# The beginning of attention: order of the first loads, reductions, casts and fillers

## The chip, the cores and the metric

The kernel runs on one core of a Trainium2 chip. A core has TensorE (PE, matrix products), VectorE (DVE), ScalarE (ACT), GpSimd (POOL) and SyncE (SP, which issues most DMAs). Each engine takes its own instructions in order; semaphores order them across engines. The metric is device time of one execution in microseconds. Before the change it was 1071.04 us, the median of three runs (1067.99 to 1071.36).

## The reference, cut to what matters

Three layers follow each other. Attention has a pooled part (q, k, v averaged over 4 neighbours) and a local part (a band of 3 neighbours to each side); then a dense layer with softplus, then a soft mixture of 8 experts.

```python
q_d, k_d, v_d = (x.reshape(B, H, Sd, 4, D).mean(axis=3) for x in (q, k, v))   # B 2, H 8, S 576, D 64
out_up = np.repeat(sm_attn(q_d, k_d, v_d), 4, axis=2)
scores = np.where(mask, scale * q @ k.T, -1e9)                                # mask: |i - j| < 4
out = out_up + softmax(scores) @ v
h = softplus(x @ w_in); x = h @ w_out                                         # 512 -> 2048 -> 512
ye = np.maximum(x @ w1[e], 0) @ w2[e]; out += P[:, e:e+1] * ye                # 8 experts, P from x @ w_gate
```

## The kernel before, in words

Heads are taken in pairs, four pairs p to a batch b. A pair's k is a tile of 128 rows (two heads of 64) by 576 positions. Its q is held twice, once for each head, with the other head's 64 rows blanked with zeros (`blank`), so that one product over 128 rows gives one head's scores. Batch 0's q lies in `q0a` (pairs 0 and 1) and `q0b` (pairs 2 and 3), places that later hold other tensors.

`load_qk` issues a pair's loads (k on SyncE's queue, q's two halves on ScalarE's queue for batch 0). `pool_qk` sums groups of 4: q by one VectorE reduction (`qd`, L250), k by two GpSimd sums (`ks`, L256, and `kd`, L258); ScalarE then scales both. `constants` loads the identity and the mask and casts them to bf16. `load_vd` loads v for pooling, in two halves, and sums each half by two instructions (`vs`, L277, and `vd`, L279), on VectorE for batch 0 and on GpSimd for batch 1. Its raw tiles `vr` share two buffers (tag `raw`) with the weights that `load_raw` loads later. `load_vw` loads v for the local windows.

The attention is cut into units. A pooled unit takes two heads and half of the pooled positions; a local unit takes 116 positions and four heads. Each has four stages: s1 scores (`pd`, or `pl` with the mask added by a product with the identity), a maximum over each row (`nm`, VectorE, L287) and exponentials (`e`, ScalarE, L290); s2 transposes (`ptd`, `ptl`) and a copy by ScalarE; s3 products with v (`pvd`, `pvl`) and the division by the sum; s4 a transpose back (`pxd`, `pxl`) and, in a local unit, the sum of both parts (`xf`) and the split into two parts of x. A unit's first scores of `pooled(0, 0, p)` use pairs 0 and 1 for p = 0 and 2, and pairs 2 and 3 for p = 1 and 3.

`emit` goes through the units; at each one it calls s1 of this unit, s2 of the unit two back, s3 of the one four back and s4 of the one six back. After these calls, counted by n, it calls `warm(1)` for n under 20 and for every fourth n up to 88. `warm` issues matmuls on a tile of zeros whose result nobody reads (fillers), 17 of them at the very start (`WARM`). Some entries in the list of units are other calls, placed by the dictionary `at`: batch 1's loads (`load_second`, at unit 1), batch 1's v and the first weights (`load_rest`, at unit 9), batch 1's pooling, the conversion of weights (`prep` and `from_double`: ScalarE `cm` L126 and `cs` L124, then VectorE), and the first products of the dense layer.

The program's order isn't the order on the engines: a planner goes through the program with simulated times, and on each engine takes the earliest instruction in the program that it holds ready. `tc.issue_after(ins)` ties what the block issues on `ins`'s engine behind `ins`; it holds nothing on other engines.

Of the kernel before, what the change touches and what calls it, by code (L numbers as in the profile page):

```python
# [19 lines left out]
DM = H * D  # L20
# [30 lines left out]
STEP = 2  # L51
WARM, JALL, JN, NJ = 17, 20, 4, 88
GP = 80
# [23 lines left out]
class Net:  # L77
# [9 lines left out]


    def constants(self):
        nc = self.nc  # L90
        self.ident = self.const.tile([P, P], F32, name="ident")
        nc.sync.dma_start(out=self.ident, in_=self.a["ident"])
        self.identb = self.atp.tile([P, P], BF16, tag="identb", name="identb", bufs=1)
        nc.vector.tensor_copy(self.identb, self.ident)
        self.mask = self.atp.tile([P, len(OFF), KW], BF16, tag="mask", name="mask", bufs=1)
        self.maskf = self.convp.tile([P, len(OFF), KW], F32, tag="cm", name="maskf", bufs=1)
        nc.sync.dma_start(out=self.maskf, in_=self.a["mask"])
        nc.vector.tensor_copy(self.mask, self.maskf)
        self.ones = self.const.tile([P, P], F32, name="ones")
        nc.gpsimd.memset(self.ones, 1.0)  # L100
# [94 lines left out]
    def warm(self, n):  # L195
# [7 lines left out]
        for _ in range(n):  # L203
            self.nc.tensor.matmul(ps, lhsT=z[:, 0], rhs=z.to_broadcast([P, 4, P]), start=True, stop=True)

    def attention_pools(self, stack):
        tc = self.tc
        self.convp = stack.enter_context(tc.tile_pool(name="conv", bufs=1, side="right"))
        self.qkp = stack.enter_context(tc.tile_pool(name="qkp", bufs=NPAIR, side="right"))
        self.vwp = stack.enter_context(tc.tile_pool(name="vwp", bufs=3, side="right"))  # L210
        self.atp = stack.enter_context(tc.tile_pool(name="atp", bufs=3, side="right"))
        self.tmp = stack.enter_context(tc.tile_pool(name="tmp", bufs=2, side="right"))
        self.psm = stack.enter_context(tc.tile_pool(name="psm", bufs=2, space=bass.MemoryType.PSUM))
        self.psa = stack.enter_context(tc.tile_pool(name="psa", bufs=6, space=bass.MemoryType.PSUM))
        self.kT, self.qd, self.kd, self.vw, self.vd, self.upT = {}, {}, {}, {}, {}, {}

    def places(self):


        q = self.hp.tile([P, 2, 2, S], F32, tag="h", name="q0a")  # L220
        x = self.xyp.tile([P, 2, 2, S], F32, tag="xy", name="q0b")
        self.qT = {(0, p): (q, x)[p // 2][:, p % 2] for p in range(NPAIR)}
        for t in (q, x):
            self.blank(t, self.nc.vector)

# [4 lines left out]
    def load_qk(self, b, p):  # L230
        nc = self.nc
        if b == 1:
            if p < NPAIR - 1:
                q = self.qkp.tile([P, 2, S], F32, tag="q", name=f"q1{p}", bufs=NPAIR - 1)
            else:
                q = self.accp.tile([P, 2, S], F32, tag="yp1", name="q13")
            self.blank(q, nc.gpsimd)
            self.qT[b, p] = q
        k = self.k1[:, p] if b == 1 else self.qkp.tile([P, S], F32, tag="k", name=f"k{p}")
        nc.sync.dma_start(out=k, in_=self.a["k"][b, p])  # L240
        self.kT[b, p] = k
        for g in range(2):
            rows = slice(g * D, (g + 1) * D)
            (nc.scalar if b == 0 else nc.sync).dma_start(out=self.qT[b, p][rows, g], in_=self.a["q"][b, p][rows])

    def pool_qk(self, b, p):

        nc = self.nc
        qd = self.atp.tile([P, 2, G], F32, tag="qd", name=f"qd{b}{p}", bufs=NPAIR)
        nc.vector.tensor_reduce(  # L250
            out=qd, in_=self.qT[b, p].rearrange("p h (g f) -> p h g f", f=POOLF), op=ALU.add, axis=AX.X
# [5 lines left out]
        kd = self.atp.tile([P, G], F32, tag="kd", name=f"kd{b}{p}", bufs=NPAIR)  # L257
        nc.gpsimd.tensor_tensor(kd, s[:, :, 0], s[:, :, 1], ALU.add)  # L258
        nc.scalar.activation(kd, kd, AF.Copy, scale=SCALE / (POOLF * POOLF))
# [8 lines left out]
    def load_vd(self, b):  # L268
# [3 lines left out]
        for hf in range(2):  # L272
            r = self.rawp.tile([GP, POOLF, DM], F32, tag="raw", name=f"vr{b}{hf}")
            nc.sync.dma_start(out=r, in_=self.a["vp"][b, hf].rearrange("p (f d) -> p f d", f=POOLF))
            s = self.convp.tile([GH, 2, DM], F32, tag=("ch", "cs")[hf], name=f"vs{b}{hf}", bufs=1)
            e = nc.vector if b == 0 else nc.gpsimd
            e.tensor_tensor(s, r[:GH, 0:2], r[:GH, 2:4], ALU.add)  # L277
            sv = s.rearrange("p f (h d) -> p f h d", h=H)
            e.tensor_tensor(vd[:, hf, :, 0:D], sv[:, 0], sv[:, 1], ALU.add)  # L279
        self.vd[b] = vd  # L280
        self.upT[b] = self.atp.tile([P, NPAIR, G], F32, tag="upT", name=f"upT{b}", bufs=2)

    def softmax_exp(self, ps, n, m, k, tag):

        nc = self.nc
        nm = self.atp.tile([m, n], F32, tag="nm" + tag, name="nm")
        nc.vector.tensor_reduce(out=nm, in_=ps, op=ALU.max, axis=AX.X, negate=True)  # L287
        e = self.atp.tile([m, n, k], F32, tag="e" + tag, name="e", bufs=3 if tag == "l" else 2)
        for j in range(n):
            nc.scalar.activation(e[:, j], ps[:, j], AF.Exp, bias=nm[:, j : j + 1])  # L290
        return e

    def pooled(self, b, hf, p):
# [4 lines left out]
        def s1():  # L298
            ps = self.psa.tile([P, 512], F32, tag="a", name="pd")[:GH, : 2 * G].rearrange("p (j k) -> p j k", j=2)
            for j in range(2):  # L300
                nc.tensor.matmul(
                    ps[:, j],
# [7 lines left out]
        def s2():  # L310
# [3 lines left out]
            for j in range(2):  # L314
                for kh in range(2):
                    nc.tensor.transpose(ps[:, j, kh], st["e"][:, j, kh * GH : (kh + 1) * GH], ident[:GH, :GH])
            pt = self.atp.tile([GH, 2, 2, GH], F32, tag="ptd", name="ptds")
            nc.scalar.copy(pt, ps)
            st["pt"] = pt

        def s3():
            ps = self.psa.tile([P, 512], F32, tag="a", name="pvd")[:GH, : 2 * DA].rearrange("p (j d) -> p j d", j=2)
            for j in range(2):
                for kh in range(2):
                    nc.tensor.matmul(
                        ps[:, j],
# [13 lines left out]
        def s4():  # L340
            ps = self.psa.tile([P, 512], F32, tag="a", name="pxd")[:, :GH]
            nc.tensor.transpose(ps, st["ul"].rearrange("p j d -> p (j d)"), ident[:GH, :GH])
            nc.scalar.copy(self.upT[b][:, p, hf * GH : (hf + 1) * GH], ps)
# [3 lines left out]
    def local(self, b, t, g):  # L347
# [6 lines left out]
        def s1():  # L354
            ps = self.psa.tile([P, 512], F32, tag="a", name="pl")[:nq, : 4 * KW].rearrange("p (j k) -> p j k", j=4)
            nc.tensor.matmul(
                ps,
# [5 lines left out]
            for j in range(4):  # L363
                nc.tensor.matmul(  # L364
                    ps[:, j],
# [7 lines left out]
        def s2():  # L373
            ps = self.psa.tile([P, 512], F32, tag="a", name="ptl")[:KW, : 4 * nq].rearrange("p (j q) -> p j q", j=4)
            for j in range(4):
                nc.tensor.transpose(ps[:, j], st["e"][:, j], ident[:nq, :nq])  # L376
            pt = self.atp.tile([KW, 4, nq], F32, tag="ptl", name="ptls")
# [3 lines left out]
        def s3():  # L381
            ps = self.psa.tile([P, 512], F32, tag="a", name="pvl")[:nq, : 4 * DA].rearrange("p (j d) -> p j d", j=4)
            for j in range(4):
                nc.tensor.matmul(  # L384
                    ps[:, j], lhsT=st["pt"][:, j], rhs=self.vw[b, t][:KW, 4 * g + j], start=True, stop=True
                )
# [10 lines left out]
        def s4():  # L397
            ps = self.psa.tile([P, 512], F32, tag="a", name="pxl")[:, : 2 * nq].rearrange("p (j q) -> p j q", j=2)
            for j in range(2):
                nc.tensor.transpose(  # L400
                    ps[:, j], st["ul"][:, 2 * j : 2 * j + 2].rearrange("p j d -> p (j d)"), ident[:nq, :nq]
# [313 lines left out]
    def run(self):  # L715
# [12 lines left out]
        self.load_qk(0, 0)  # L728
        self.load_qk(0, 1)
        self.pool_qk(0, 0)  # L730
        self.pool_qk(0, 1)
        for p in (2, 3):
            self.load_qk(0, p)
            self.pool_qk(0, p)
        self.constants()
        self.load_vd(0)
        for t in range(3):
            self.load_vw(0, t)

        def emit(items, rest):  # L740

            live = []
            n = 0
            tail = [y for x in zip([None] * (3 * STEP), rest) for y in x] + rest[3 * STEP :]
            for it in [*items, *tail]:
                if callable(it):
# [15 lines left out]
        def load_second():  # L762

            self.k1 = self.hp.tile([P, NPAIR, S], F32, tag="h", name="k1")
            for p in range(NPAIR):
                self.load_qk(1, p)

        def load_rest():
            self.load_vd(1)
            self.load_raw(1)  # L770

# [229 lines left out]
```

## Time and profile before

| | us |
|---|---|
| median of three runs | 1071.04 |
| the profiled execution | 1068.01 |
| its span, first to last instruction | 1066.2 |
| TensorE busy in the span | 1043.2 (98%) |
| VectorE busy | 784.9 (74%) |
| ScalarE busy | 435.0 (41%) |
| GpSimd busy | 169.8 (16%) |

The busy time of TensorE holds the fillers too, and ends of matmuls are modelled, so 98% is not 98% of useful work. In slices of a fortieth of the span (26.7 us), only the first shows TensorE well under full, and DMA engines are at nine tenths in the first slice and at six tenths in the second. Attention, with the dense layer's first products among it, lasts to about 148 us.

### The profile page before, as it was taken

The numbers are of one execution on the slowest core, as the hardware profiler recorded it, in microseconds if no ns is written. First come the engines' busy times: TensorE is split into PE (matmuls) and PEld (weight loads), VectorE is DVE, ScalarE is ACT, GpSimd is POOL, SyncE is SP. The second block draws the span as 40 slices with busy tenths as digits, with TensorE's granted clock in tenths as the row PEclk, the third lists the DMA queues.
The fourth block names the chain that finished last, engine by engine and source line by source line (L and its number), as shares of the span: only waits on it lengthen the run. The fifth ranks groups of instructions, "written<-read, shape, count | busy, mean of one in ns | idle before, by whom it ended". The sixth has DMA issues, their size and how long they took to land.

```text
span 1066.2 us, 16125 instructions
## 1 busy us (share of the span) xinstructions
PE 1043.2 (98%) x6421; PEld 959.5 (90%) x6421; DVE 784.9 (74%) x1466; ACT 435.0 (41%) x815; POOL 169.8 (16%) x218
## 2 busy tenths in 40 slices
PE   7899999999999999999999999999999999999998
PEld 4889999999998899898989989898998989899896
DVE  6798699999987787874947658494765848576572
ACT  3777687767644443231413324141332414133130
POOL 3456300002112210211102021120201112020000
PEclk9999999999999999999999999999999999999999
DMA  9642032222111221111211111121111112110003
GB/s 231 177 134 83 1 120 79 79 80 80 41 40 40 79 80 40 40 41 40 65 56 40 41 40 41 40 80 40 40 40 40 41 40 79 40 41 1 1 2 89
DMA packets 13035, 63.99 MB, mean 60 GB/s; under 512 B 1760, under 2 KB 2016, under 8 KB 6496
## 3 DMA queue, kind: packets, MB, share of 16 engines
q1 hardware_dynamic: 12320, 61.79, 18.1%
q10 hardware_dynamic: 640, 1.18, 0.5%
q8 instruction: 50, 0.82, 0.3%
q14 instruction: 25, 0.20, 0.1%
HBM read 60.60 MB, written 2.36 MB: 59 GB/s over the span
## 4 chain that ended last, share of the span: by engine, by line
PE 87%; DVE 4%; ACT 3%; POOL 1%; issue 0%; ACTq 0%; DVEq 0%
PE po L586 37%; PE pu L537 33%; PE ph L444 8%; PE py L486 7%; PE pvl L384 1%; PE pl L364 0%; ACT cm L126 0%; ACT e L455 0%; DVE ch L130 0%; POOL x L419 0%; ACT r L458 0%; DVE a L168 0%; PE ptl L376 0%; ACT e L454 0%; PE pg L635 0%
## 5 line engine op out<-in xcount | busy, mean ns | idle before, releaser
L537 PE MATMUL pu<-T,a 128*128 128x320 f32 (+1 forms) x2688 | 354.3, 293 | 1.3 <-DVE yp L498 1.3
L537 PEld LDWEIGHTS pu<-T,a 128*128 128x128 f32 x2688 | 351.4, 188 | 2.9 <-issue 1.6
L608 DVE SCALAR_TENSOR_TENSOR acc<-po,prob,acc 128x512 f32<-128x512 f32 x126 | 94.1, 749 | 173.5 <-PE po L586 173.5
L586 PE MATMUL po<-w,h 128*128 128x512 f32 x960 | 221.3, 390 | 0.0
L586 PEld LDWEIGHTS po<-w,h 128*128 128x128 f32 x960 | 180.0, 188 | 37.3
L188 ACT CAST w<-raw 128x1024 fp32r<-128x1024 f32 x32 | 33.4, 1052 | 271.5 <-PE po L586 271.5
L586 PE MATMUL po<-w,h0a 128*128 128x512 f32 x576 | 142.4, 391 | 0.6 <-DVE w L189 0.6
L157 POOL TENSOR_TENSOR s<-raw 128x256 f32<-128x256 f32 x32 | 28.7, 897 | 676.2 <-DVE a L168 472.8
L586 PEld LDWEIGHTS po<-w,h0a 128*128 128x128 f32 x576 | 107.3, 188 | 22.5 <-DVE w L189 1.0
L444 PE MATMUL ph<-x,w 128*128 128x384 f32 x576 | 104.1, 337 | 1.3 <-ACT yp L496 1.3
L486 PE MATMUL py<-h,w 128*128 128x384 f32 x576 | 103.8, 336 | 1.3 <-DVE h L465 0.9
L486 PEld LDWEIGHTS py<-h,w 128*128 128x128 f32 x576 | 99.8, 188 | 2.0 <-DVE h L465 1.4
L444 PEld LDWEIGHTS ph<-x,w 128*128 128x128 f32 x576 | 99.6, 188 | 1.7 <-ACT yp L496 1.6
L549 ACT ACTIVATE h<-c 128x320 fp32r<-128x320 f32 x128 | 58.6, 469 | 79.7 <-DVE c L560 79.7
L550 DVE SCALAR_TENSOR_TENSOR h<-c,h 128x320 fp32r<-128x320 f32 x128 | 68.3, 541 | 0.3
L560 DVE TENSOR_TENSOR c<-v,pu 128x256 f32<-128x256 f32 (+1 forms) x128 | 58.0, 453 | 10.8 <-PE pu L537 7.8
L549 ACT ACTIVATE h0a<-c 128x256 fp32r<-128x256 f32 x96 | 37.4, 417 | 50.9 <-DVE c L560 50.6
L189 DVE TENSOR_TENSOR w<-raw,w 128x1024 fp32r<-128x1024 f32 x32 | 39.0, 1221 | 22.1 <-ACT w L188 22.1
L586 PE MATMUL po<-w,h0b 128*128 128x512 f32 x192 | 54.3, 389 | 0.0
L586 PEld LDWEIGHTS po<-w,h0b 128*128 128x128 f32 x192 | 36.0, 188 | 7.5
L558 ACT COPY p<-pu 128x256 f32<-128x256 f32 (+1 forms) x64 | 25.1, 393 | 36.8 <-PE pu L537 35.2
L550 DVE SCALAR_TENSOR_TENSOR h0a<-c,h0a 128x256 fp32r<-128x256 f32 x96 | 39.2, 421 | 0.9 <-ACT h0a L549 0.6
(141 smaller groups left out, 1250.1 us busy)
## 6 DMA issues: line engine op xcount, KB each, us to landing
raw<-in_w SPq DMA_DIRECT2D x48, 1024.0 KB, 4.9
vw<-in_vw SPq DMA_DIRECT2D x10, 260.0 KB, 2.9
vr<-in_vp SPq DMA_DIRECT2D x4, 640.0 KB, 9.4
k<-in_k SPq DMA_DIRECT2D x8, 288.0 KB, 6.2
out<-acc SPq DMA_DIRECT2D x5, 256.0 KB, 2.0
q<-in_q SPq DMA_DIRECT2D x8, 144.0 KB, 6.4
out<-acc SPq DMA_DIRECT2D x8, 128.0 KB, 2.3
q0a<-in_q ACTq DMA_DIRECT2D x4, 144.0 KB, 6.5
```

The lines of the kernel that those rows point to most:

```text
L157: nc.gpsimd.tensor_tensor(s[:, 0], a21, a22, ALU.add)
L188: nc.scalar.copy(w[:, 0], raw)
L189: nc.vector.tensor_tensor(w[:, 1], raw, split(w[:, 0]), ALU.subtract)
L444: nc.tensor.matmul(ps[:, i], lhsT=wv[:, a, k, fo : fo + P], rhs=x[:, b, k], start=(n == 0), stop=(n == 3 * KD - 1),)
L486: nc.tensor.matmul(ps[:, a], lhsT=w[:, i, d * P : (d + 1) * P], rhs=h[:, j, f], start=(n == 0), stop=(n == 3 * NFT - 1),)
L537: nc.tensor.matmul(ps, lhsT=w[:, x, a, k], rhs=t[:, y, b, k], start=(m == 0), stop=(m == 5))
L549: act = nc.scalar.activation(hi, src, AF.Relu)
L550: dve = nc.vector.scalar_tensor_tensor(lo, src, 0.0, split(hi), ALU.max, ALU.subtract)
L558: nc.scalar.copy(to, ps)
L560: nc.vector.tensor_tensor(to, src, ps, ALU.add)
L586: nc.tensor.matmul(ps, lhsT=self.h[s, i, f][:, at * P : (at + 1) * P], rhs=w[:, j], start=(n == 0), stop=(n == 3 * NFT - 1),)
L608: nc.vector.scalar_tensor_tensor(acc, ps, pe, acc, ALU.mult, ALU.add)
```

## The change: what it does

Loads: pairs 0 and 1 first, then the identity, pairs 2 and 3 and the mask; only pair 0's q stays on ScalarE's queue. Blanks of `q0b` and the two casts go from VectorE to GpSimd; the casts are tied behind the pooling of k of pair 1, and batch 1's blanks behind the mask's cast. A function `head` writes out the first four units by hand: s1 and s2 of units 0 and 1 with fillers behind each, then the pooling of pairs 2 and 3 (tied behind the last maximum and the last exponential), v's loads, s1 of units 2 and 3 (tied behind the last transpose), and the sum of v's first half tied behind their maximum. The sum of the second half is issued in unit 0's s3, tied behind the last maximum and the first half's sum. Every filler of `emit` is tied behind the last matmul issued (`keep`). `WARM` goes from 17 to 24, and `load_second` from unit 1 to unit 4.

```diff
-WARM, JALL, JN, NJ = 17, 20, 4, 88
+WARM, JALL, JN, NJ = 24, 20, 4, 88
+HEAD = 6, 5, 4
@@ constants
-        nc.vector.tensor_copy(self.identb, self.ident)
+        nc.gpsimd.tensor_copy(self.identb, self.ident)
-        nc.vector.tensor_copy(self.mask, self.maskf)
+        self.masked = nc.gpsimd.tensor_copy(self.mask, self.maskf)
@@ warm
+    def keep(self, n):
+        with self.tc.issue_after(self.pe.ins):
+            self.warm(n)
@@ places
-        for t in (q, x):
-            self.blank(t, self.nc.vector)
+        for t, engine in ((q, self.nc.vector), (x, self.nc.gpsimd)):
+            self.blank(t, engine)
@@ load_qk
-            (nc.scalar if b == 0 else nc.sync).dma_start(out=self.qT[b, p][rows, g], in_=self.a["q"][b, p][rows])
+            (nc.scalar if b == p == 0 else nc.sync).dma_start(out=self.qT[b, p][rows, g], in_=self.a["q"][b, p][rows])
@@ pooled, s3
+            if (b, hf, p) == (0, 0, 0):
+                with self.tc.issue_after(self.top.ins), self.tc.issue_after(self.vsum.ins):
+                    self.sum_vd(0, 1)
@@ run
         self.load_qk(0, 0)
         self.load_qk(0, 1)
+        self.load_ident()
+        self.load_qk(0, 2)
+        self.load_qk(0, 3)
+        self.load_mask()
         self.pool_qk(0, 0)
         self.pool_qk(0, 1)
-        for p in (2, 3):
-            self.load_qk(0, p)
-            self.pool_qk(0, p)
-        self.constants()
-        self.load_vd(0)
-        for t in range(3):
-            self.load_vw(0, t)
+        with self.tc.issue_after(self.pooled_k.ins):
+            self.constants()
+
+        def pool_rest():
+            with self.tc.issue_after(self.top.ins), self.tc.issue_after(self.exp.ins):
+                for p in (2, 3):
+                    self.pool_qk(0, p)
+            self.load_vd(0)
+            for t in range(3):
+                self.load_vw(0, t)
+
+        def head(units):
+            for k in range(2):
+                for u in units[:2]:
+                    u[k]()
+                self.keep(HEAD[k])
+            pool_rest()
+            with self.tc.issue_after(self.pe.ins):
+                for u in units[2:4]:
+                    u[0]()
+            self.keep(HEAD[2])
+            with self.tc.issue_after(self.top.ins):
+                self.sum_vd(0, 0)
@@ emit
-            live = []
-            n = 0
+            head(items[:4])
+            live = items[3::-1]
+            n = 4 + 2
-                            self.warm(1)
+                            self.keep(1)
@@ load_second
-            for p in range(NPAIR):
-                self.load_qk(1, p)
+            with self.tc.issue_after(self.masked.ins):
+                for p in range(NPAIR):
+                    self.load_qk(1, p)
@@ after the table of places
+        at[4] = at.pop(1) + at.get(4, [])
```

## Rows read from the trace of the kernel before

**Rows 1.** Chain that ended last, in order of time: start us, us, what.
```profile
148.34 8.60 PE ph L444 x48
...
1037.91 24.52 PE po L586 x108
```

**Rows 2.** Busy us (instructions) by stretch, granted clock PEclk, DMA share, GB/s.
```profile
25.40:42.20 16.80, 16.12 (x169) 15.37 (x170) 13.13 (x35) 11.98 (x40) 9.00 (x9) 1.00 0.81 212
...
42.16:45.94 3.78, 0.00 (x0) 0.00 (x0) 1.74 (x6) 2.74 (x5) 2.73 (x6) 1.00 0.94 370
45.94:50.00 4.06, 4.06 (x27) 3.91 (x27) 2.74 (x7) 2.72 (x11) 1.32 (x2) 0.58 0.02 6
...
50.00:70.00 20.00, 17.83 (x175) 17.07 (x173) 18.78 (x50) 17.83 (x45) 11.68 (x11) 1.00 0.44 146
70.00:100.00 30.00, 29.01 (x249) 27.66 (x248) 27.40 (x67) 23.68 (x66) 17.41 (x18) 1.00 0.28 89
```

**Rows 3.** Fillers alone (line 204) by stretch: PE, PEld, PEclk, DMA share, GB/s.
```profile
25.40:42.20 16.80, 0.00 (x0) 0.00 (x0) 1.00 0.81 212
...
70.00:100.00 30.00, 0.77 (x2) 0.19 (x2) 1.00 0.28 89
```

**Rows 4.** Busy time by stretch, for its last two columns: DMA share, GB/s.
```profile
0.00:20.30 20.30, 16.65 (x73) 8.37 (x73) 11.62 (x15) 6.83 (x15) 9.25 (x23) 0.92 0.94 212
20.30:35.92 15.62, 12.83 (x126) 11.11 (x126) 12.39 (x31) 11.21 (x38) 3.39 (x7) 1.00 1.03 262
```

**Rows 5.** Timeline of VectorE: start us, us, line, operation, tiles [idle before <-releaser].
```profile
20.30 1.22 DVE L277 TENSOR_TENSOR vs<-vr 72x1024 f32<-72x1024 f32 x1 [1.97 <-DMA vr<-in_vp]
21.44 1.34 DVE L250 TENSOR_REDUCE qd<-q0b 128x288 f32<-128x1152 f32 x1
22.70 0.68 DVE L279 TENSOR_TENSOR vd<-vs 72x512 f32<-72x512 f32 x1
```

**Rows 6.** Timeline of TensorE's matmuls, 23 to 46 us.
```profile
23.38 1.68 PE L204 MATMUL pz<-z 128*128 128x512 bf16 x7
...
25.57 0.68 PE L325 MATMUL pvd<-vd,ptds 72*72 72x65 f32 x8
...
41.74 0.42 PE L400 MATMUL pxl<-ident,ull 116*128 116x116 f32 x2 [0.57 <-DVE rsd L333]
45.94 0.37 PE L356 MATMUL pl<-mask,identb 116*116 116x488 bf16 x1 [3.79 <-ACT e L290]
```

**Rows 7.** Timelines of GpSimd, SyncE's queue, VectorE and ScalarE, 35 to 46 us.
```profile
35.92 4.67 POOL L277 TENSOR_TENSOR vs<-vr 72x1024 f32<-72x1024 f32 x2 [3.78 <-DMA vr<-in_vp]
38.30 2.67 SPq L108 DMA_DIRECT2D raw<-in_w  x2
39.65 0.44 DVE L287 TENSOR_REDUCE nm<-pd 72x2 f32<-72x288 f32 x1
43.20 1.13 ACT L126 ACTIVATE cm<-raw 128x1024 f32<-128x1024 f32 x1 [4.00 <-DMA raw<-in_w]
45.25 0.65 ACT L290 ACTIVATE e<-pd,nm 72x144 f32<-72x144 f32 x2
```

**Rows 8.** DMA issues: tiles, queue, count, KB each, median us to landing.
```profile
vr<-in_vp SPq DMA_DIRECT2D x4, 640.0 KB, 9.4
k<-in_k SPq DMA_DIRECT2D x8, 288.0 KB, 6.2
...
q0a<-in_q ACTq DMA_DIRECT2D x4, 144.0 KB, 6.5
maskf<-in_mask SPq DMA_DIRECT2D x1, 183.0 KB, 6.5
ident<-in_ident SPq DMA_DIRECT2D x1, 64.0 KB, 6.9
```

**Rows 9.** GpSimd's blanks, and its copies of x: ns min/median/max, first and last start.
```profile
L228 POOL MEMSET q<- x8: 571/572/572, 1.1 to 5.4; 64x576 f32 x8
...
L420 POOL TENSOR_TENSOR x<-xf,x x18: 335/674/4186, 44.1 to 109.8; 128x232 fp32r<-128x232 f32 x8, 128x72 fp32r<-128x72 f32 x2, 128x160 fp32r<-128x160 f32 x2, 128x224 fp32r<-128x224 f32 x2
```

More of the change, by code (lines that the diff above doesn't have):

```diff
@@ L86, in __init__, with load_ident, load_mask @@
         self.next_raw = 0
+    def load_ident(self):
+        self.ident = self.const.tile([P, P], F32, name="ident")
+        self.nc.sync.dma_start(out=self.ident, in_=self.a["ident"])
+    def load_mask(self):
+        self.maskf = self.convp.tile([P, len(OFF), KW], F32, tag="cm", name="maskf", bufs=1)
+        self.nc.sync.dma_start(out=self.maskf, in_=self.a["mask"])
     def constants(self):
         nc = self.nc
-        self.ident = self.const.tile([P, P], F32, name="ident")
-        nc.sync.dma_start(out=self.ident, in_=self.a["ident"])
         self.identb = self.atp.tile([P, P], BF16, tag="identb", name="identb", bufs=1)
-        nc.vector.tensor_copy(self.identb, self.ident)
+        nc.gpsimd.tensor_copy(self.identb, self.ident)
         self.mask = self.atp.tile([P, len(OFF), KW], BF16, tag="mask", name="mask", bufs=1)
-        self.maskf = self.convp.tile([P, len(OFF), KW], F32, tag="cm", name="maskf", bufs=1)
-        nc.sync.dma_start(out=self.maskf, in_=self.a["mask"])
-        nc.vector.tensor_copy(self.mask, self.maskf)
+        self.masked = nc.gpsimd.tensor_copy(self.mask, self.maskf)
         self.ones = self.const.tile([P, P], F32, name="ones")
@@ L214, in attention_pools @@
         self.psa = stack.enter_context(tc.tile_pool(name="psa", bufs=6, space=bass.MemoryType.PSUM))
-        self.kT, self.qd, self.kd, self.vw, self.vd, self.upT = {}, {}, {}, {}, {}, {}
+        self.kT, self.qd, self.kd, self.vw, self.vd, self.upT, self.vr = {}, {}, {}, {}, {}, {}, {}
     def places(self):
@@ L249, in pool_qk @@
         qd = self.atp.tile([P, 2, G], F32, tag="qd", name=f"qd{b}{p}", bufs=NPAIR)
-        nc.vector.tensor_reduce(
+        self.pooled_q = nc.vector.tensor_reduce(
             out=qd, in_=self.qT[b, p].rearrange("p h (g f) -> p h g f", f=POOLF), op=ALU.add, axis=AX.X
@@ L257, in pool_qk @@
         kd = self.atp.tile([P, G], F32, tag="kd", name=f"kd{b}{p}", bufs=NPAIR)
-        nc.gpsimd.tensor_tensor(kd, s[:, :, 0], s[:, :, 1], ALU.add)
+        self.pooled_k = nc.gpsimd.tensor_tensor(kd, s[:, :, 0], s[:, :, 1], ALU.add)
         nc.scalar.activation(kd, kd, AF.Copy, scale=SCALE / (POOLF * POOLF))
@@ L274, in load_vd, with sum_vd @@
             nc.sync.dma_start(out=r, in_=self.a["vp"][b, hf].rearrange("p (f d) -> p f d", f=POOLF))
[L275 to L279, printed above, removed]
+            self.vr[hf] = r
         self.vd[b] = vd
         self.upT[b] = self.atp.tile([P, NPAIR, G], F32, tag="upT", name=f"upT{b}", bufs=2)
+    def sum_vd(self, b, hf):
+        nc, vd, r = self.nc, self.vd[b], self.vr[hf]
+        s = self.convp.tile([GH, 2, DM], F32, tag=("ch", "cs")[hf], name=f"vs{b}{hf}", bufs=1)
+        e = nc.vector if b == 0 else nc.gpsimd
+        e.tensor_tensor(s, r[:GH, 0:2], r[:GH, 2:4], ALU.add)
+        sv = s.rearrange("p f (h d) -> p f h d", h=H)
+        self.vsum = e.tensor_tensor(vd[:, hf, :, 0:D], sv[:, 0], sv[:, 1], ALU.add)
     def softmax_exp(self, ps, n, m, k, tag):
@@ L286, in softmax_exp @@
         nm = self.atp.tile([m, n], F32, tag="nm" + tag, name="nm")
-        nc.vector.tensor_reduce(out=nm, in_=ps, op=ALU.max, axis=AX.X, negate=True)
+        self.top = nc.vector.tensor_reduce(out=nm, in_=ps, op=ALU.max, axis=AX.X, negate=True)
         e = self.atp.tile([m, n, k], F32, tag="e" + tag, name="e", bufs=3 if tag == "l" else 2)
         for j in range(n):
-            nc.scalar.activation(e[:, j], ps[:, j], AF.Exp, bias=nm[:, j : j + 1])
+            self.exp = nc.scalar.activation(e[:, j], ps[:, j], AF.Exp, bias=nm[:, j : j + 1])
         return e
@@ L300, in s1 @@
             for j in range(2):
-                nc.tensor.matmul(
+                self.pe = nc.tensor.matmul(
                     ps[:, j],
@@ L315, in s2 @@
                 for kh in range(2):
-                    nc.tensor.transpose(ps[:, j, kh], st["e"][:, j, kh * GH : (kh + 1) * GH], ident[:GH, :GH])
+                    self.pe = nc.tensor.transpose(ps[:, j, kh], st["e"][:, j, kh * GH : (kh + 1) * GH], ident[:GH, :GH])
             pt = self.atp.tile([GH, 2, 2, GH], F32, tag="ptd", name="ptds")
@@ L324, in s3 @@
                 for kh in range(2):
-                    nc.tensor.matmul(
+                    self.pe = nc.tensor.matmul(
                         ps[:, j],
@@ L341, in s4 @@
             ps = self.psa.tile([P, 512], F32, tag="a", name="pxd")[:, :GH]
-            nc.tensor.transpose(ps, st["ul"].rearrange("p j d -> p (j d)"), ident[:GH, :GH])
+            self.pe = nc.tensor.transpose(ps, st["ul"].rearrange("p j d -> p (j d)"), ident[:GH, :GH])
             nc.scalar.copy(self.upT[b][:, p, hf * GH : (hf + 1) * GH], ps)
@@ L355, in s1 @@
             ps = self.psa.tile([P, 512], F32, tag="a", name="pl")[:nq, : 4 * KW].rearrange("p (j k) -> p j k", j=4)
-            nc.tensor.matmul(
+            self.pe = nc.tensor.matmul(
                 ps,
@@ L363, in s1 @@
             for j in range(4):
-                nc.tensor.matmul(
+                self.pe = nc.tensor.matmul(
                     ps[:, j],
@@ L375, in s2 @@
             for j in range(4):
-                nc.tensor.transpose(ps[:, j], st["e"][:, j], ident[:nq, :nq])
+                self.pe = nc.tensor.transpose(ps[:, j], st["e"][:, j], ident[:nq, :nq])
             pt = self.atp.tile([KW, 4, nq], F32, tag="ptl", name="ptls")
@@ L383, in s3 @@
             for j in range(4):
-                nc.tensor.matmul(
+                self.pe = nc.tensor.matmul(
                     ps[:, j], lhsT=st["pt"][:, j], rhs=self.vw[b, t][:KW, 4 * g + j], start=True, stop=True
@@ L399, in s4 @@
             for j in range(2):
-                nc.tensor.transpose(
+                self.pe = nc.tensor.transpose(
                     ps[:, j], st["ul"][:, 2 * j : 2 * j + 2].rearrange("p j d -> p (j d)"), ident[:nq, :nq]
@@ L729, in run @@
         self.load_qk(0, 1)
+        self.load_ident()
+        self.load_qk(0, 2)
+        self.load_qk(0, 3)
+        self.load_mask()
         self.pool_qk(0, 0)
         self.pool_qk(0, 1)
-        for p in (2, 3):
-            self.load_qk(0, p)
-            self.pool_qk(0, p)
-        self.constants()
-        self.load_vd(0)
-        for t in range(3):
-            self.load_vw(0, t)
+        with self.tc.issue_after(self.pooled_k.ins):
[19 more added lines that the diff above has]
+                self.sum_vd(0, 0)
         def emit(items, rest):
-            live = []
-            n = 0
+            head(items[:4])
+            live = items[3::-1]
+            n = 4 + 2
             tail = [y for x in zip([None] * (3 * STEP), rest) for y in x] + rest[3 * STEP :]
-            for it in [*items, *tail]:
+            for it in [*items[4:], *tail]:
                 if callable(it):
@@ L764, in load_second @@
             self.k1 = self.hp.tile([P, NPAIR, S], F32, tag="h", name="k1")
-            for p in range(NPAIR):
-                self.load_qk(1, p)
+            with self.tc.issue_after(self.masked.ins):
+                for p in range(NPAIR):
+                    self.load_qk(1, p)
         def load_rest():
             self.load_vd(1)
+            for hf in range(2):
+                self.sum_vd(1, hf)
             self.load_raw(1)
```

## The prediction, made before the changed kernel ran

> **What bounds the kernel now.** I read the chain of waits first: from 148.3 us on it is TensorE alone, product after product, up to the last matmul [rows 1]. What this change touches lies before that, so a gain must be TensorE time that is saved before 148 us. The busy time by stretch tells where such time is to be had [rows 2]. From 25.4 to 42.2 us TensorE is busy for 16.12 of 16.80 us at full granted clock. Then it does nothing from 42.16 to 45.94, and after that gap the granted clock is 0.58 for 4.06 us. From 50 us it is all but full again: 17.83 of 20, 29.01 of 30. So TensorE binds from 25.4 us on, except for one gap of 3.78 us.
>
> Before 25.4 us TensorE mostly runs fillers (matmuls on zeros that nobody reads), seven of them in a row still at 23.38 [rows 6]. What it waits for is in the timelines. The DMA engines carry 212 GB/s to 20.30 us and 262 GB/s to 35.92, without a pause between the two [rows 4]. VectorE gets the second half of v at 20.30, and before it may finish that sum it takes the pooling of q's last pair (21.44, 1.34 us), then the sum (22.70), then maxima; the first attention products pvd follow at 25.57 [rows 5, 6].
>
> The gap has another cause [rows 7]. Weights go into two buffers that v's raw tiles of batch 1 held before. Those land at 35.92, GpSimd sums them, SyncE issues the weight load at 38.30, and it lands at 43.20. ScalarE is in order: the weight's conversion cm stands in front of the exponentials e, whose maxima nm were ready at 40.09. TensorE's next scores pl need the bank that e frees, and start at 45.94. So the head ends not in one bound but in two: the compute chain up to 25.57, and a stream of loads whose end does not depend on that chain.
>
> **The change, part by part.** The sum is made against the profiled execution: 1068.01 us, of which the span is 1066.2. The runs shown have a median of 1071.04 (1067.99 to 1071.36); the profiled one is 3.0 below it, at their lower end.
>
> *Loads by first use.* The bytes are the same. Ahead of v's second half stand k of four pairs, q of four pairs in two halves, identity, mask and v: 4 x 288 + 8 x 144 + 64 + 183 + 2 x 640 = 3831 KB = 3.92 MB [rows 8]. Before, 20.3 us x 212 GB/s = 4.30 MB had moved when it landed, since two queues shared the engines and some of what stands behind was among it. With nearly all on SyncE's queue 3.92 MB are through 0.38 MB earlier, at 212 GB/s 1.8 us: 18.5 us. Bounds: 18.5, and 20.3 if order changes nothing. Six q loads go from ScalarE's queue to SyncE's; their issue is hidden by engines that are already full. Q's first two pairs come before k's last two, so the reduction of pair 1 can start once 2 x 288 + 4 x 144 KB = 1.18 MB are in, at 212 GB/s 5.6 us; I take 7.5, since a stream has a start. That is not on the path: v is.
>
> *First maxima and exponentials ahead; v's sums late.* With q's pairs all in before v, the reduction of 1.34 us and the maxima no longer stand between v's landing and its sum. What is left is 1.22 + 0.68 us after the landing [rows 5]: 20.4 us, or 22.2 from the late bound. I take 21.1 for the first pvd, the early end and something for two pinned orders, so 4.5 us earlier than 25.57 (bounds 3.4 and 5.2).
>
> *Casts and one blank on GpSimd, batch 1's blanks behind the mask.* VectorE loses two blanks and two casts in a stretch where it waits anyway: nothing. GpSimd's eight blanks of 0.572 us [rows 9] go behind the mask. The mask is in after 2.55 MB, at 212 GB/s 12.0 us; with its casts they then run until about 18, when GpSimd has nothing else that is due: nothing, and up to the fourth case below if loads should wait for them.
>
> *Fillers held in place.* This is the part that costs. Before, no filler ran between 25.4 and 42.2 us [rows 3]: nothing held them back, so the planner put them into earlier idle time. `keep` ties each to the matmul ahead of it. One stands behind every stage call up to the 19th and every fourth up to the 84th. The full stretch has 169 matmuls [rows 2], at about five to a call 33 calls; seven calls came before it, so it ends with call 40. Calls 9 to 40 bring 11 + 6 = 17 fillers, and calls 44 to 84 behind it 11. Seven in a row took 1.68 us [rows 6] and one alone 0.77 / 2 = 0.385 [rows 3], so one more behind another costs (1.68 - 0.385) / 6 = 0.216 us. So 17 cost 3.7 us, and 11 cost 2.4; bounds nothing (all in idle time) and 6.1 together. After 50 us there are 2.2 + 1.0 us of idle time [rows 2], which I let hide half of the 11: 1.2 us.
>
> The page "TensorE: Matmul & The Clock Gate" of the Trainium skill (Part 1) says that the clock is held down until the array is busy and falls again in idle gaps; by that rule held fillers earn their time, up to the half clock behind the gap (4.06 us at 0.58 would be 2.35: 1.7 us). The rows speak against it here: the clock was 1.00 over the whole stretch without one filler, and in the gap TensorE is stopped by its next matmul, which a filler ahead of it doesn't shorten. By the rule the sum below would be 1.7 lower.
>
> *Where it meets the weight load.* TensorE comes to the place of the gap at 42.16 - 4.5 + 3.7 = 41.4 us. The load stream must still carry the same bytes, so v of batch 1 lands at about 35.9, the weights at about 43.2. What comes earlier waits longer, unless the planner now puts more of the attention ahead of cm on ScalarE. I expect a part of it: the exponentials that stood behind cm, and one copy, since they are ready sooner against a load that isn't. That lets TensorE go on into the gap with the scores that wait for a bank and the products that wait for the copy. Bounds: nothing, and the whole gap of 3.78 us; I take 2.3, a little over the middle, since work that ScalarE has done before 43.20 is work that TensorE can follow.
>
> Sum: 0 from the head by itself (the gap takes it), -2.3 from work in the gap, +1.2 from later fillers: -1.1, so 1066.9 against 1068.01. I say 1067.0.
>
> **The rivals.**
>
> *The gap goes altogether.* The planner moves the conversion behind all attention work that is ready, and TensorE never stops. Then 0.8 us from the earlier arrival, 3.78 from the gap and 1.7 from the clock are won, and 11 fillers cost their full 2.4, since no idle time hides them: -3.9, 1064.1 us. For it: in program order the attention units of that place come ahead of the weight's preparation, and cm is first only because they weren't ready when the planner's clock thought the weight was there. Against it: the head start reaches that place shrunk to 0.8 us by fillers, which the planner sees as well, and cm would have to move by more than 3 us (43.20 against 40.09) [rows 7].
>
> *The order stays.* The conversion keeps its place, TensorE resumes at 45.94 as before, and only later fillers are left: +1.2 to +2.4, 1069.2 to 1070.4 us. For it: the chain that ends the gap (35.92, 38.30, 43.20) has no link in the changed code. Against it: a planner's order seldom survives a shift of its inputs.
>
> *GpSimd holds up the second batch's loads: slower.* The q tiles of batch 1 are blanked behind the mask now. If SyncE's queue waits for these blanks and the DMA engines run dry, every microsecond lost there moves the weights behind 43.20. The blanks end near 18 us, v in front of them lands at 18.5 to 20.3, so it decides only from over 2 us of delay on. GpSimd can be that late: one of its copies of x took 4.186 us against a median of 0.674 [rows 9], and one such stretch is 3.5 us. With two the blanks end at 25, and with v's local windows still to carry the engines are dry for about 3 us; with later fillers +1.2 that is +4.2: 1072.2 us. Against it: a blank fills the 64 rows of a tile that its load leaves alone, so nothing in the data makes the one wait for the other.
>
> The page "SBUF — State Buffer" (Who interferes with whom) of the Trainium skill says that a GpSimd instruction that reads that memory and a VectorE instruction with two inputs there exclude each other, while one that only writes isn't touched; by it the casts can be held up but the blanks can't, and this case would end below 1070. No run here has shown it for a blank.
>
> **How the numbers follow.** The forecast (gap partly filled): 0.35, own range 1065 to 1069. Gap gone: 0.33, 1062 to 1066. Order stays: 0.18, 1068.5 to 1070.5. Loads late: 0.14, from 1070 on. About 0.3%, 3.2 us, is what can be told from no change, so by the level of the profiled execution the bounds are 1064.8 and 1071.2. Faster: most of the second case and some of the first, 0.27 + 0.10 = 0.37. Slower: 0.11 of the fourth, 0.05 from fillers that nothing hides: 0.16. Within: 0.47. The range for 8 in 10 is 1062.5 to 1071.5; its upper end also takes in that two of the runs shown lie 3 us above the profiled one.
>
> **What would show it.** Right, if in the changed kernel the reduction of q's pair 1 starts near 7.5 us and v's second sum by 19 to 20; if the first pvd starts near 21; if fillers stand singly between 21 and 42 us, at granted clock 1.00 before and behind them; if the weight's cm still waits for its load to about 43; and if TensorE's gap ahead of 46 us is there, but shorter. The second case shows as no gap over 1 us after 25 us and clock 1.00 between 46 and 50. The fourth shows as DMA share well under 1 somewhere from 18 to 30 us. Wrong altogether, if pvd starts no earlier than 24 us, or if TensorE reaches its steady products other than about a microsecond before 148.3 us.

## The result and the profile after

The changed kernel took 1075.51 us (median of six, 1074.14 to 1078.32), the kernel before, beside it, 1068.91 (1065.02 to 1071.36). The ratio is 1.0075, interval 1.0055 to 1.0096: about 0.75% slower, where 1067.0 and most likely no change had been forecast. The profiled execution is the slowest of the six (1078.32 us, span 1076.5, mean granted clock 0.987 against 0.990 to 0.994 in the others), so its half clock is on the long side.

The loss is there before the steady part. This row of the chain of waits answers to the last of [rows 1]:

```profile
1048.21 24.52 PE po L602 x108
```

The same products start 10.3 us later, and 10.3 us is all that the span grew by. The head itself came early, as VectorE's timeline shows (start, us, line, tiles; idle before and its releaser in brackets; compare [rows 5]):

```profile
6.55 2.61 DVE L259 TENSOR_REDUCE qd<-q0a 128x288 f32<-128x1152 f32 x2 [3.01 <-DMA q0a<-in_q]
...
18.13 1.22 DVE L292 TENSOR_TENSOR vs<-vr 72x1024 f32<-72x1024 f32 x1 [0.40 <-DMA vr<-in_vp]
...
19.64 0.68 DVE L294 TENSOR_TENSOR vd<-vs 72x512 f32<-72x512 f32 x1
```

V's second half is in by 18.13. TensorE's timeline has a first product with the sum of v's first half at 17.78, and from 20.37 on products with both, 5.2 us before 25.57 [rows 6]. Then it loses the lead:

```profile
17.78 0.34 PE L341 MATMUL pvd<-vd,ptds 72*72 72x65 f32 x2 [0.37 <-DVE vd L294]
...
20.37 0.60 PE L341 MATMUL pvd<-vd,ptds 72*72 72x65 f32 x6
...
26.33 0.38 PE L358 MATMUL pxd<-ident,uld 72*128 72x72 f32 x1 [2.14 <-ACT ptls L394]
...
45.13 1.03 PE L392 MATMUL ptl<-ident,e 116*122 116x116 f32 x4 [3.87 <-ACT ptds L331]
...
88.87 3.70 PE L460 MATMUL ph<-x,w 128*128 128x384 f32 x12 [1.62 <-DVE l L479]
...
110.09 0.69 PE L502 MATMUL py<-h,w 128*128 128x384 f32 x1 [3.02 <-DVE h L481]
```

There are four gaps. The first two are ScalarE's, in its timeline:

```profile
25.16 0.68 ACT L269 ACTIVATE k<-k 128x576 f32<-128x576 f32 x1 [2.19 <-POOL ks L265]
25.75 0.53 ACT L394 COPY ptls<-ptl 122x464 f32<-122x464 f32 x1
...
42.65 1.12 ACT L131 ACTIVATE cm<-raw 128x1024 f32<-128x1024 f32 x1 [3.92 <-DMA raw<-in_w]
```

At 25.16 the scaling of batch 1's k, which waits for its load, stands in front of a copy that TensorE needs: this wait is new. It isn't in every execution: the first and the seventh experiment below have the same order up to there, and in their profiles it is 0.67 and 0.70 us. At 42.65 it is the weight's conversion, as before (43.20 in [rows 7]). The other two gaps are new, and they begin on VectorE and GpSimd:

```profile
85.36 2.35 DVE L478 TENSOR_TENSOR l<-l,r 128x384 f32<-128x384 f32 x1
...
88.28 0.54 DVE L479 SCALAR_TENSOR_TENSOR l<-ph,l 128x384 f32<-128x384 f32 x1
...
107.92 2.12 DVE L481 TENSOR_TENSOR h<-l,h 128x384 fp32r<-128x384 f32 x1
```

```profile
84.48 2.82 POOL L142 TENSOR_TENSOR w<-cs,ch 128x1024 fp32r<-128x1024 f32 x1 [4.57 <-DVE ch L140]
...
106.97 2.66 POOL L142 TENSOR_TENSOR w<-cs,ch 128x1024 fp32r<-128x1024 f32 x1
```

VectorE's l and h, parts of softplus, take 0.54 to 0.56 us in most other places. Here each lasts until 0.41 us after GpSimd's multiply has ended: 85.36 + 2.35 = 87.71 against 84.48 + 2.82 = 87.30, and 110.04 against 109.63. So VectorE's instruction seems to have stood still until the multiply was all but over; call this a meeting. The page "SBUF — State Buffer" (Who interferes with whom) of the Trainium skill says that a VectorE instruction with two inputs there and a GpSimd instruction that reads there exclude each other; these two pairs agree.

Busy us by stretch (TensorE, its weight load, VectorE, ScalarE, GpSimd, each with its count; granted clock, DMA share, GB/s) shows what stands behind the gaps; compare [rows 2]:

```profile
25.40:42.20 16.80, 14.93 (x118) 13.37 (x118) 10.35 (x22) 9.43 (x31) 10.76 (x12) 0.82 0.79 228
45.13:50.00 4.87, 4.87 (x23) 4.52 (x24) 1.31 (x6) 2.60 (x10) 1.41 (x2) 0.50 0.00 0
50.00:70.00 20.00, 19.25 (x149) 17.90 (x148) 16.70 (x41) 14.24 (x38) 9.29 (x8) 0.78 0.40 132
70.00:100.00 30.00, 28.38 (x238) 27.36 (x237) 23.69 (x62) 22.09 (x62) 12.71 (x19) 0.94 0.20 63
```

and, for TensorE alone:

```profile
24.00:32.00 8.00, 5.86 (x33) 0.57 1.06 260
45.00:59.00 14.00, 13.12 (x66) 0.51 0.24 77
89.00:93.00 4.00, 4.00 (x18) 0.57 0.02 6
110.00:114.00 4.00, 3.91 (x23) 0.58 0.02 4
```

118 matmuls stand where 169 were. At each of the four gaps the clock falls to the lower of its two levels (1.2 GHz), for a while: (1 - clock) x length is 3.4, 6.9, 1.7 and 1.7 us. Before it was 1.7 behind the one gap (45.94 to 50) and 1.7 at 12 to 16 us, among the fillers. The held fillers alone, by stretch [rows 3]:

```profile
25.40:42.20 16.80, 4.91 (x12) 0.82 0.79 228
...
70.00:100.00 30.00, 1.77 (x5) 0.94 0.20 63
```

### The profile page after: what moved, and what is told of

The parts are those of the page before. It is cut to its first block, busy times and chain, and to the rows that moved or that the text cites. A ratio compares the mean times of both kernels' runs of the same rounds, so it can differ in the third digit from the quotient of the medians.

```text
span 1076.5 us, 16145 instructions
## 1 busy us (share of the span) xinstructions
PE 1053.6 (98%) x6437; PEld 969.3 (90%) x6437; DVE 784.4 (73%) x1462; ACT 435.3 (40%) x815; POOL 169.4 (16%) x222
## 4 chain that ended last, share of the span: by engine, by line
PE 86%; DVE 8%; DMA 3%; ACT 1%; issue 1%; SPq 0%; POOL 0%; DVEq 0%; ACTq 0%; POOLq 0%
PE po L602 36%; PE pu L553 32%; PE ph L460 7%; PE py L502 6%; DMA vr<-in_vp 2%; PE pvl L400 1%; PE pl L380 1%; DVE h L481 1%; DVE l L478 1%; DVE r L477 1%; DMA q<-in_q 1%; DMA raw<-in_w 1%; PE ptl L392 1%; DVE ch L135 1%; DVE l L479 1%
```

## The experiments

Theories at the start: the loss is half clock behind the early gap ("clock theory"), or fillers that displace work ("filler theory"). A third came up on the way: the two later gaps, which the meetings open.

"Lost clock" below is (1 - mean granted clock) x span, worked out for every run and averaged: 5.2 us for the kernel before (30 runs), 9.5 for the changed one (6). Ratios are to the kernel before on the same chip, 1068.1 us for the first four and 1068.8 and 1068.7 for the others. Differences to the changed kernel's 1075.51 us go across these sets of runs; the kernel before, 1068.9 us beside it, differs by up to 0.8 us among them.

**Four single edits of the changed kernel.** First, 18 fillers more, in the gap ahead of 45 us alone:

```diff
                         u[k]()
                         n += 1
+                        for at_unit, stage, extra in [(12, 0, 18)]:
+                            if it is order[at_unit] and k == stage:
+                                self.keep(extra)
```

> The changed kernel with 18 more fillers held behind the scores of unit 12, just ahead of the transposes for which TensorE waited from 41.1 to 45.13 us; its other matmuls keep their order. Clock theory (what the change loses is the half clock behind its gaps, 45 to 59 us here): 18 x 0.216 = 3.9 us of useless work fill the gap, TensorE goes on at 45.1 us at full clock, and some 5 to 7 us come back: 1069 to 1071 us against 1075.5. Filler theory (each held filler costs its 0.216 us): 3.9 us slower, 1079. Waiting theory (only the gap counts): no change, 1075.5.

1070.86 us, ratio 1.0028 (1.0014 to 1.0042), lost clock 4.6. The order of the other matmuls is the same; with useless work in the gap it is 4.6 us faster. TensorE's timeline, then busy us by stretch:

```profile
37.79 4.05 PE L209 MATMUL pz<-z 128*128 128x512 bf16 x18
42.77 0.61 PE L392 MATMUL ptl<-ident,e 116*122 116x116 f32 x4 [0.93 <-ACT ptds L331]
```

```profile
46.00:59.00 13.00, 11.48 (x103) 10.22 (x102) 12.82 (x34) 10.73 (x30) 8.57 (x8) 1.00 0.51 162
80.00:115.00 35.00, 30.30 (x254) 28.99 (x253) 27.00 (x68) 22.95 (x69) 12.76 (x16) 0.95 0.14 46
```

The clock stays full behind the filled gap. The two later gaps remain, 1.62 and 3.02 us, which is why the last stretch has 30.30 busy us of 35.

Second, the first weight's conversion tied behind the exponentials issued last:

```diff
+                if n == 0:
+                    st.enter_context(self.tc.issue_after(self.exp.ins))
                 self.prep(n)
```

> The changed kernel with the first weight's conversion tied behind the last exponentials issued before it in the program; TensorE's order is the same up to 74 us. Clock theory and waiting theory: ScalarE no longer stops for the weight load at 38.7 us, the gap of 3.9 us goes and with it the 6.8 us that the half clock behind it costs: 1065 to 1068 us by the clock theory, 1071 to 1072 if only the gap counts. Filler theory: no change, 1075.5.

1064.67 us, ratio 0.9969 (0.9957 to 0.9982): faster than both kernels. The gap at 45 is gone, and so are the later two.

Third, the scaling of batch 1's k (all of `pool_qk`) tied in the same way:

```diff
-            at.setdefault(11 + p, []).append(lambda p=p: self.pool_qk(1, p))
+            def later(p=p):
+                with self.tc.issue_after(self.exp.ins):
+                    self.pool_qk(1, p)
+            at.setdefault(11 + p, []).append(later)
```

> The changed kernel with ScalarE's scalings of batch 1's k tied behind the last exponentials issued, so that they don't stand in front of batch 0's copies at 21.8 and 25.2 us. The gap of 2.1 us at 24.2 and the half clock behind it (3.4 us) go. The weight load still ends at about 42.7 us, so TensorE waits there longer. Clock theory: nearly all given back, 1073 to 1076 us. If the weight load did not bind: 5.5 us faster, 1070. Filler theory: 1075.5.

1066.92 us, ratio 0.9986 (0.9972 to 1.0000). TensorE's timeline, and its later stretch:

```profile
43.43 1.03 PE L392 MATMUL ptl<-ident,e 116*122 116x116 f32 x4 [8.15 <-ACT ptds L331]
```

```profile
80.00:115.00 35.00, 33.33 (x294) 32.05 (x293) 27.10 (x74) 26.77 (x80) 16.87 (x18) 1.00 0.16 53
```

This was a miss for the clock theory: the gap doubled to 8.15 us, since TensorE gets there earlier and the weights don't, and yet the kernel is 8.6 us faster than the changed one. The stretch from 80 to 115 us is full again.

Fourth, fillers not held:

```diff
-                            self.keep(1)
+                            self.warm(1)
```

> The changed kernel with the fillers of the unit loop no longer held behind a matmul (those of the head stay). Filler theory (28 of them cost 0.216 us each in a full stretch): up to 6 us faster, 1069.5 to 1072. Clock theory: TensorE comes to the weight gap some 3.5 us earlier and waits as much longer, the clock falls as before: 1074 to 1077.

1065.75 us, ratio 0.9981 (0.9967 to 0.9994), better than either theory said. The gap at 43.64 is still 3.88 us; again no later gaps. So without held fillers behind the head the change is worth 2.4 us, and holding them there costs 9.8. Three different edits each give back 8.6 to 10.8 us; they can't each remove a cost of their own as large. What they have in common is that the later gaps don't come.

**Which cost is it?** The next four runs tell apart the fillers, the early gap and the later gaps. The kernel before with held fillers only (`keep(1)` for `warm(1)`):

> The kernel before with one part of the change: its fillers are held behind the last matmul issued, nothing else. Held fillers as the cost by themselves (some 28 behind 25 us at 0.216 us each): 1071 to 1074 us beside 1068.1. The half clock as the cost (fillers only delay what then meets the same late load): 1067.5 to 1069.5, the gap ahead of 46 us shorter by what the fillers take ahead of it, and no gap over 1 us between 80 and 115 us. If the fillers shift the planner's order so that later gaps come, they show at 80 to 115 us and it is over 1072.

1074.79 us, ratio 1.0064 (1.0048 to 1.0080): nearly the whole loss, without the head's new order. The order of its engines parts from that of the kernel before at 23 us on VectorE, 31 on ScalarE, 53 on GpSimd and 70 on TensorE. GpSimd's, VectorE's and TensorE's timelines show the same pair of meetings:

```profile
80.14 2.83 POOL L137 TENSOR_TENSOR w<-cs,ch 128x1024 fp32r<-128x1024 f32 x1 [4.57 <-DVE ch L135]
...
101.06 2.66 POOL L137 TENSOR_TENSOR w<-cs,ch 128x1024 fp32r<-128x1024 f32 x1
```

```profile
81.02 2.37 DVE L466 TENSOR_TENSOR l<-l,r 128x384 f32<-128x384 f32 x1
...
102.01 2.12 DVE L469 TENSOR_TENSOR h<-l,h 128x384 fp32r<-128x384 f32 x1
```

```profile
84.54 2.35 PE L448 MATMUL ph<-x,w 128*128 128x384 f32 x12 [1.62 <-DVE l L467]
...
104.18 0.44 PE L490 MATMUL py<-h,w 128*128 128x384 f32 x1 [3.02 <-DVE h L469]
```

The gaps are as long as in the changed kernel, but the clock stays full behind the first of them:

```profile
84.54:88.54 4.00, 4.00 (x33) 3.91 (x34) 2.33 (x9) 4.00 (x12) 0.00 (x0) 1.00 0.02 4
```

The kernel before with the conversion's tie only (the second edit):

> The kernel before with the first weight's conversion tied behind the exponentials issued last, without the change. If the wait behind the load (3.78 us of gap and 1.7 us of half clock) is TensorE time of its own: 1062.5 to 1065 beside 1068.1, no gap over 1.5 us at 42 to 46 us. If the gain of the second experiment needs the earlier head: 1067 to 1069.

1069.48 us, ratio 1.0003 (0.9988 to 1.0018). Its gap at 45.06 shrank to 2.42 us, but new ones came, among them one of 1.87 at 104.06, just after VectorE's r was stretched to 2.61 us beside a multiply of GpSimd that began at 100.55.

The changed kernel with the third and fourth weights' last multiply on VectorE. Every engine keeps the changed kernel's order up to the place of the first meeting, 85 us there:

```diff
-        e = nc.gpsimd if n < NFT else nc.vector
+        e = nc.gpsimd if n < 2 else nc.vector
```

> The changed kernel with the last multiply of the third and fourth weights on VectorE instead of GpSimd, so that no GpSimd multiply runs beside VectorE at 85 and 107 us. Two later gaps as the main cost (1.62 + 3.02 us of idle TensorE, 2 x 1.7 us of half clock behind them): 1067 to 1069, no gap at 80 to 115 us. The early gap and the half clock behind it (45 to 59 us) as the main cost: 1073 to 1075, since that stays. VectorE as the bound there (2 x 1.2 us more on it): 1075 or more.

1068.76 us, ratio 1.0004 (0.9991 to 1.0016), lost clock 4.0: 6.75 us of the loss is gone, with the head and its fillers as they were. VectorE's timeline, and TensorE's:

```profile
82.34 0.54 DVE L478 TENSOR_TENSOR l<-l,r 128x384 f32<-128x384 f32 x1
```

```profile
42.73 1.03 PE L392 MATMUL ptl<-ident,e 116*122 116x116 f32 x4 [5.59 <-ACT ptds L331]
```

The l takes its 0.54 us, and no gap over 1 us stands between 80 and 115. The early gap is there, even longer. So the meetings are the main cost, not the early gap. Not all of the 6.75 us is theirs, though. These are TensorE's products just ahead of the first meeting, in the changed kernel and here:

```profile
85.69 0.93 PE L400 MATMUL pvl<-vw,ptls 122*116 122x65 f32 x8
```

```profile
81.55 0.93 PE L400 MATMUL pvl<-vw,ptls 122*116 122x65 f32 x8
```

Of the 9.0 us between the two profiles (spans 1076.5 and 1067.5), 4.1 lie ahead of these products, where the order is the same: the weight's conversion starts at 42.65 in one and 40.25 in the other. Behind them lie 4.9 us, which the edit gives back.

The second, third and fourth edits together (conversion's tie, scaling's tie, fillers not held):

> The changed kernel with the three single edits of before together: fillers not held, scaling of batch 1's k and the first weight's conversion each tied behind the exponentials issued last. If each takes away a wait of its own (2.1 us at 26, 3.9 us at 45, 1.7 us of half clock behind each): 1060 to 1063. If all three only shift the order so that the same two later gaps don't come, they don't add up: 1064 to 1067.

1060.77 us (1060.21 to 1061.91), ratio 0.9931 (0.9918 to 0.9944): the best here, 0.7% under the kernel before and 14.7 us under the changed one. Busy by stretch:

```profile
24.00:60.00 36.00, 31.89 (x301) 29.46 (x300) 28.83 (x73) 27.39 (x79) 22.11 (x23) 1.00 0.58 179
...
80.00:115.00 35.00, 33.04 (x278) 32.00 (x277) 27.23 (x69) 24.10 (x70) 12.13 (x17) 1.00 0.15 47
```

301 matmuls stand in the first stretch where the changed kernel has 195 (at clock 0.72) and the kernel before 282. No gap between 24 and 148 us is over 1.6 us, and the clock stays full. Yet this kernel has a meeting too (VectorE's, GpSimd's and TensorE's timelines):

```profile
89.14 2.65 DVE L478 TENSOR_TENSOR l<-l,r 128x384 f32<-128x384 f32 x1
```

```profile
89.03 2.35 POOL L142 TENSOR_TENSOR w<-cs,ch 128x1024 fp32r<-128x1024 f32 x1 [5.45 <-DVE cs L139]
```

```profile
92.16 1.02 PE L400 MATMUL pvl<-vw,ptls 122*116 122x65 f32 x8 [1.16 <-DVE xf L422]
```

So a meeting need not cost much: TensorE waits for 1.16 us behind this one, at full clock.

**Is it the fillers or the order?** The fifth kernel with the seventh's edit:

> The kernel before with held fillers (the fifth experiment), and the last multiply of the third and fourth weights on VectorE instead of GpSimd; its engines take the same order as in the fifth up to about 65 us. If held fillers cost only because they shift the planner's order so that VectorE's softplus work stands beside GpSimd's multiplies: 1067 to 1070, no gap at 80 to 110 us. If the 28 fillers cost TensorE time themselves: 1071.5 to 1074 even without those gaps.

1068.96 us, ratio 1.0002 (0.9988 to 1.0017). The held fillers run as in the fifth, the meetings are gone, and so is the whole cost (5.8 us). The two profiles are 7.0 us apart (spans 1071.8 and 1064.8), 4.9 of them behind the products just ahead of the meeting (81.35 and 79.22), as in the seventh. Half clock in the first 28 us, among the held fillers, is in both. Busy by stretch, with no gap over 1 us behind 58 us:

```profile
80.00:115.00 35.00, 33.46 (x292) 31.91 (x292) 27.78 (x77) 25.58 (x77) 10.90 (x16) 1.00 0.15 47
```

The rival that this multiply is simply better on VectorE has no run of its own (the kernel before with that edit alone). The same stretch of the kernel before leaves it little:

```profile
80.00:115.00 35.00, 33.48 (x295) 32.28 (x294) 27.59 (x74) 26.58 (x79) 18.62 (x18) 1.00 0.19 64
```

TensorE idles for 1.5 us in all there, at full clock, and none of VectorE's r, l and h takes over 0.88 us. In the twelfth experiment below the same edit goes with a longer time, not a shorter one.

The kernel before with both ties:

> The kernel before with the two ties of the eighth experiment (scaling of batch 1's k and the first weight's conversion behind the exponentials issued last); its fillers were never held, and nothing else of the change is in it. If the 1060.8 us of the eighth needs the change's earlier head: 1066 to 1070. If the two ties alone give it: 1061 to 1064.

1072.36 us, ratio 1.0043 (1.0027 to 1.0059), slower than either case. Its early gap is gone, but VectorE's r, 0.54 us elsewhere, met two multiplies of GpSimd (77.87 and 97.05 us) (VectorE's timeline, then TensorE's):

```profile
78.72 1.93 DVE L461 SCALAR_TENSOR_TENSOR r<-r,e 128x384 f32<-128x384 f32 x1
...
97.27 2.54 DVE L461 SCALAR_TENSOR_TENSOR r<-r,e 128x384 f32<-128x384 f32 x1
```

```profile
80.97 0.44 PE L316 MATMUL ptd<-ident,e 72*72 72x72 f32 x4 [1.72 <-DVE uld L337]
...
100.51 0.35 PE L342 MATMUL pxd<-ident,uld 72*128 72x72 f32 x1 [3.00 <-DVE uld L337]
```

The eighth kernel without fillers behind the head (`JALL, NJ = 7, 0`):

> The eighth experiment without any filler behind the head (about 12 of them ran at 25 to 45 us, 4.07 us of TensorE). Fillers as displaced work: 1057 to 1060. Fillers in idle time and clock kept by the work itself: 1060 to 1062. Fillers needed for the clock, or the planner's order upset without them: 1063 or more, with half clock in the granted-clock column before 50 us or gaps over 1.5 us.

1066.56 us, ratio 0.9977 (0.9962 to 0.9992): 5.8 us slower than the eighth. Gaps of 2.98, 2.04 and 1.87 us (at 41.90, 65.46 and 81.66) came back with half clock behind them. The last follows a meeting (VectorE's r, 1.94 us at 79.47, beside a multiply at 78.62). How much of the 5.8 us each cause made isn't told apart here.

The eighth with the seventh's edit:

> The eighth experiment with the last multiply of the third and fourth weights on VectorE. In the eighth no gap over 1.2 us stands behind 50 us, so if the gaps were all that the GpSimd multiplies cost: within 1 us of 1060.8. If stretched VectorE work costs in small waits too: 1057 to 1059. If VectorE is the bound: over 1062.

1064.40 us (1061.30 to 1064.54), ratio 0.9951 (0.9934 to 0.9969). The time is that of the last case, but the profile doesn't show VectorE as the bound: that execution is 1061.3, like the eighth, with full clock throughout. The other four are 3 us longer at 0.996 to 0.998. Why they lost clock isn't known, since only one was profiled.

## Why the prediction was wrong, point by point

**What bounds the kernel.** Right as far as it went: TensorE binds from 25 us on, and the weight load sets the gap. It went only to the gap. Behind 50 us I read TensorE's idle time, 2.2 + 1.0 us, as cover for fillers, and did not look for what would open new gaps there. The chain behind 148.3 us isn't TensorE alone either: near 190 and from 295 to 322 us it is mostly ScalarE and VectorE. It made no difference to the sum, since 10.1 of the 10.3 us are lost ahead of the second of these stretches (rows of the chain before, then of the changed kernel's):

```profile
296.92 3.22 DVE a L168 x3
```

```profile
307.04 3.22 DVE a L173 x3
```


**Loads by first use; first maxima ahead.** Right: the second half of v by 18.13 (18.5 to 20.3 expected), products with it at 20.37 (21.1 expected).

**Fillers held in place: this step failed.** I priced them as TensorE time, 3.7 + 2.4 us with half of the second hidden. 12 stand in the first stretch (17 expected), and in the ninth experiment held fillers cost nothing on balance (1.0002, with an early gap of 0.96 us in place of 3.78). The sum had no term for what holding does to the planner: its order moves on all engines far behind the head, so that l and h of the dense layer's first products stand beside GpSimd's multiplies of the third and fourth weights. Without these meetings the median falls by 5.8 us in the kernel before (1074.79 to 1068.96) and by 6.75 in the changed one (1075.51 to 1068.76), and 4.9 us of either lie behind the place of the first meeting in the profiles: most of the loss of 6.6 us. Lost clock fell by 5.5 us in the changed kernel (9.5 to 4.0), but no more than 3.4 of that stood behind the two gaps. The rest lies ahead of them, where the order is the same, and why the runs differ there stays open.

**"By the rule held fillers earn their time."** I weighed the page "TensorE: Matmul & The Clock Gate" (Part 1) of the Trainium skill against a stretch that was at full clock anyway and dropped its rule. Eighteen fillers in the gap kept the clock at 1.00 and gave 4.6 us, so its rule holds where the gap is. The change's fillers aren't there: they stand between matmuls that run anyway. Half clock behind the early gap, which I took as 1.7 us, was 6.9 in the profiled execution.

**Where it meets the weight load.** The expected work in the gap (2.3 us) didn't come: 3.87 us against 3.78. That the head's lead is swallowed there was right, and the third experiment shows it at its purest (8.15 us). The scaling of k in front of a copy, 2.14 us at 26.33 in this profile, I had not seen; half clock from 24 to 32 us goes with it.

**The rivals.** "The order stays" (1069.2 to 1070.4) was right on the early gap and 5 us short, because the order changed behind it. "The gap goes altogether" (1064.1) is what the second experiment built by a tie: 1064.67. The slower rival named GpSimd, but its loads: q's blanks ended by 18.2, and batch 1's v landed at 33.6, earlier than the 35.92 of [rows 7]. Where GpSimd and VectorE did meet was at 85 and 108 us instead of 20, and not over blanks or casts.

**The range** ended at 1071.5 because every case was priced within the first 50 us, plus fillers.

## What to carry to other kernels

Where a planner writes the order, an edit is paid for wherever the order shifts: read the whole stretch that it plans, not the edited part, and look for VectorE instructions that grew beside GpSimd ones. Idle TensorE time is paid a second time when the clock falls behind it, so first take away the waits (here two ties on ScalarE and fillers left free) and only then bring work forward: the same head that lost 0.75% with held fillers gains 0.7% in the eighth experiment.

## What the runs showed of the hardware that had not been expected

Every VectorE instruction that was stretched to 1.9 us or more ended 0.41 to 0.43 us after GpSimd's multiply: l and h in the changed kernel, the first and the fifth experiment, r in the sixth, tenth and eleventh, l in the eighth. In the changed kernel, the first and the fifth experiment the gaps of TensorE behind the meetings were the same too, 1.62 and 3.02 us, though the fifth has the head of the kernel before.

What the clock does behind a gap isn't fixed. Behind the gap of 1.62 us it was 0.57 for 4 us in the changed kernel, and stayed at 1.00 in the first and the fifth experiment. The fall was 14 us long behind 3.87 us in the changed kernel's profile, 4 behind 3.78 before, 8 (42 to 50) behind 3.88 in the fourth, and absent behind gaps of 1.55 and 1.15 us in the eighth. What makes these differences stays open.
